# Queries of three rounds before the first weights, value tiles in their used rows, and half a mask in a scheduled place: one change to the start of a three-layer kernel

## The chip, the cores and the metric

The kernel runs on one core of a Trainium2 chip. Its five engines (TensorE, called PE in the profile; VectorE, DVE; ScalarE, ACT; GpSimd, POOL; SyncE, SP) each take their own list of instructions in order and wait for each other with semaphores. All loads and stores of the stretch looked at here are issued by SP on one DMA queue that feeds 16 DMA engines. The metric is the time of one execution in microseconds of the device; lower is better.

## What is computed

```python
scores = scale * np.matmul(q, k.transpose(0, 1, 3, 2))          # batch 4, 8 heads, 576 tokens, head size 64
mask_local = (rel >= 0) & (rel < 32)                            # heads 0 to 3
mask_strided = (rel >= 0) & (pos[None, :] % 32 == pos[:, None] % 32)   # heads 4 to 7
...
x = softmax(where(mask, scores, -1e9)) @ v                      # 2304 tokens x 512
h = x @ w_in; r = np.maximum(h, 0.0)                            # 512 x 2048
x = (s * (r * r) + b) @ w_out                                   # 2048 x 512
logits = x @ w_gate; e_idx = np.argmax(logits, axis=1)          # one of 8 experts for each token
out[mask] = gate_w * eom * (np.maximum(x[mask] @ w1[e], 0.0) @ w2[e])
```

## The kernel before

**Units and rounds.** The 2304 tokens are cut into five units: unit 0 has 256 tokens, units 1 to 4 have 512. Attention comes in 30 rounds (`GROUPS`). A round of kind L holds blocks of 64 local queries with 96 keys each; kinds P and T hold the strided heads (P the first residue rows of a batch, T the rest). A round is: scores on PE into a pair of PSUM banks (line 574 puts the mask there as a product with the identity, line 579 adds query times key), the maximum on DVE (line 605), for the first nine rounds one exponential for each block on ACT (line 613), the sum's reciprocal and the division on DVE (lines 627 to 630), transposes on PE (line 648), a copy on ACT (line 654), the product with the values on PE (lines 685 and 687), and two halves of the result, high on ACT (line 714) and low on DVE (line 731), in the tile `xsl`, which is the x of the next layer. Unit 0 needs rounds 0 (L), 1 (L) and 2 (P). Unit 1 needs rounds 3 (L), 4 (L), 5 (T), 6 (T), 7 (L) and 8 (P).

**The dense layers.** A step of unit u and slice fc is 12 products of the first layer into `h` (line 855) and, one step later, 12 products of the second layer into four accumulators (line 885). Between them a chain squares the rectified `h` on ACT (lines 819, 824, 832) and leaves a low half to DVE (line 834). The first steps are: five of unit 0, whose second-layer products come after all five; then ten of unit 1; then the rest of unit 0. So unit 1's first five steps use the ten weight tiles that unit 0's five have used already.

**Weights.** A weight tile arrives as 64-bit numbers (`raw`, 512 KB, line 753). DVE puts together a 32-bit number in three steps (lines 791, 794, 797), the high half is copied by ACT (line 765) or DVE (line 767), and DVE makes the low half (line 778). The order is `WSEQ`: five tiles of the first layer, five of the second, then the rest.

**What sets the order.** A planner (`Order`) runs while the program is built: it keeps a clock for each engine, takes the piece of work that could start first by its own cost figures (with small bonuses), and so writes one list for each engine. The chip only follows these lists. A spawned piece with `after=True` may not be planned before the spawning piece has finished on the planner's clock. SP's list too comes from it: `load_qkv` issues `LOADS` one after the other (k = 0 is queries with keys, k = 1 values), `load_w64` the weights, and `FIRST_LOADS` weaves the first of both by small delays (q a query tile, v a value tile, w a weight). Loads share a pool of 32 slots (`t_w`); in the list a load also waits for the one eight places before it. Where the planner expects PE to be idle it puts in products on a tile of zeros (`warm`, line 1571, and `filler`, line 1582); they read and write nothing that counts.

**The start.** `prep` makes the identity, the local mask and, in a loop over two parts, the two strided masks of batch 0 (part 0 for kind P, part 1 for kind T) on POOL, each followed by a copy on ACT (line 461).

Of the kernel before, what the change touches and what calls it, by code (L numbers as in the profile page):

```python
# [10 lines left out]
AF = mybir.ActivationFunctionType  # L11
# [8 lines left out]
NT, DM, DFF, E, DFE = B * S, H * D, 2048, 8, 1024  # L20
# [14 lines left out]
P = 128  # L35
# [3 lines left out]
LK = QB + STRIDE  # L39
# [51 lines left out]
def steps():  # L91
# [6 lines left out]
GROUPS = [("L", 0, 0, 2), ("L", 0, 2, 2), ("P", 0, 0, 4),  # L98
# [4 lines left out]


def part_of(g):

    kind, b = GROUPS[g][0:2]
    late = kind == "T"
    return FIRST[b] * late, CLS if late else FIRST[b], RES[b][late]


def dims(g):

    if GROUPS[g][0] == "L":
        return QB, LK
    j0, j1, r = part_of(g)
    return r * (j1 - j0), QB if GROUPS[g][0] == "P" else r * j1
# [22 lines left out]
MB = [(QB if b < 3 else RES[b][0] * FIRST[b], RES[b][1] * CLS) for b in range(B)]  # L140
# [23 lines left out]


WQ, WV = 1024, 768
LOADS = [(0, 0), (1, 0), (0, 1), (2, 0), (1, 1), (3, 0), (2, 1), (3, 1)] + [(g, k) for g in range(4, len(GROUPS)) for k in range(2)]
FIRST_LOADS = "qwqvwqvwqvwvw"
LATE_Q = [k / 1000 for k, x in enumerate(FIRST_LOADS) if x in "qv"]
LATE_W = [k / 1000 for k, x in enumerate(FIRST_LOADS) if x == "w"]  # L170


def widths(g):
    kind, b, i0, n = GROUPS[g]
    qw, w = dims(g)
    if kind == "L":
        return 2 * (n * QB + n * QB + STRIDE), n * 2 * P
    if kind == "P":
        return 2 * 2 * n * QB, n * P
    return 2 * (n * qw + QB - qw + n * w), n * 2 * P  # L180
# [118 lines left out]
def op(*engs, waits=(), dep=True, on=(), late=0.0):  # L299
    return engs, waits, dep, on, late  # L300
# [6 lines left out]
def body(ctx, tc, qkv, w12, moe_s, moe_b, wg, e12, out):  # L307
    nc = tc.nc
# [10 lines left out]
    at = at_ctx.enter_context(tc.tile_pool(name="at", bufs=2))  # L319
# [15 lines left out]
    mh = wp.tile([P, sum(MB[0])], F32R, name="mh", tag="w")  # L335
# [14 lines left out]
    wgt = const.tile([P, KD, 4 * E], F32, name="wgt")  # L350
# [3 lines left out]
    wt = const.tile([P, E], F32, name="wt")  # L354
# [11 lines left out]
    o = Order()  # L366
# [71 lines left out]
    def prep():  # L438
        nc.vector.memset(ones, 1.0)
        nc.vector.memset(zero.bitcast(F32), 0.0)  # L440
        one = mx.tile([P, P], F32, name="one", tag="r", bufs=NR)
        nc.gpsimd.memset(one, 0.0)
        nc.gpsimd.affine_select(out=one, in_=one, pattern=[[-1, P]], compare_op=ALU.not_equal,
                                fill=1.0, base=0, channel_multiplier=1)
        nc.scalar.activation(out=ident_r, in_=one, func=AF.Copy)
        nc.scalar.activation(out=minus_r, in_=one, func=AF.Copy, scale=-1.0)
        nc.vector.tensor_reduce(out=pick, in_=one.rearrange("p (k e) -> p e k", e=4 * E), axis=AX.X, op=ALU.add)
        mf = mx.tile([P, 2 * LK + sum(MB[0])], F32, name="mf", tag="r", bufs=NR)
        loc = mf[:, 0:2 * LK].rearrange("p (i k) -> p i k", i=2)
        nc.gpsimd.memset(loc, 0.0)  # L450
        for a in range(0, P, QB):
            nc.gpsimd.affine_select(out=loc[a:a + QB], in_=loc[a:a + QB], pattern=[[0, 2], [-1, LK]], compare_op=ALU.is_ge,
                                    fill=NEG, base=STRIDE, channel_multiplier=1)
            nc.gpsimd.affine_select(out=loc[a:a + QB], in_=loc[a:a + QB], pattern=[[0, 2], [1, LK]], compare_op=ALU.is_gt,
                                    fill=NEG, base=0, channel_multiplier=-1)
        nc.gpsimd.memset(loc[:, 0, 0:STRIDE], NEG)
        nc.scalar.activation(out=mk[:, 0:2 * LK], in_=mf[:, 0:2 * LK], func=AF.Copy)
        for k in range(2):
            make_masks(0, (k,), mf[:, 2 * LK:])
            a, b = k * MB[0][0], MB[0][0] + k * MB[0][1]  # L460
            nc.scalar.activation(out=mh[:, a:b], in_=mf[:, 2 * LK + a:2 * LK + b], func=AF.Copy)
        nc.gpsimd.memset(wgt, 0.0)
        nc.gpsimd.iota(wt, pattern=[[-1, E]], base=E, channel_multiplier=0, allow_small_or_imprecise_dtypes=True)
        o.clock["DVE"] = 1.7
        o.clock["DMA"] = 1.4
        o.clock["POOL"] = 5.5
        o.clock["ACT"] = 5.5
        o.clock["PE"] = 1.7
        ev_mk.t = 4.2
        ev_mp.t = 5.8  # L470
        ev_mb[0].t = 8.5


    def make_masks(b, parts, m):

        for k in parts:
            j0, j1, r, w = ((0, FIRST[b], RES[b][0], MB[b][0]), (FIRST[b], CLS, RES[b][1], MB[b][1]))[k]
            c = k * MB[b][0]
            v, nj = m[:, c:c + w], j1 - j0
            used = r * j1  # L480
            nc.gpsimd.memset(v[:, 0:used], 0.0)
            if used < w:
                nc.gpsimd.memset(v[:, used:], NEG)
            for a in range(0, P, QB):
                x = v[a:a + QB, 0:used].rearrange("p (r j) -> p r j", j=j1)
                for pattern, base, sign in (([[-nj, r], [-1, j1]], j0, 1), ([[nj, r], [0, j1]], nj - 1, -1)) + ((([[-nj, r], [0, j1]], 0, 1),) if j0 else ()):
                    nc.gpsimd.affine_select(out=x, in_=x, pattern=pattern, compare_op=ALU.is_ge, fill=NEG, base=base, channel_multiplier=sign)

    ev_mb = [Ev() for _ in range(B)]
    ev_mp = Ev()  # L490
    ev_md = [Ev() for _ in range(B)]

    def masks(b):
        yield op(("POOL", 8.0), waits=[ev_k[0]] if b == 1 else [ev_md[b - 1]])
        t = at_pool.tile([P, sum(MB[1])], F32, name="xt", tag="xt", bufs=1)
        make_masks(b, (0, 1), t)
        yield op(("ACT", 0.35))
        nc.scalar.activation(out=xm[:, 0:sum(MB[b])], in_=t[:, 0:sum(MB[b])], func=AF.Copy)
        o.set(ev_mb[b])
        if b + 1 < B:  # L500
            o.spawn(masks(b + 1))

    ev_k = [Ev() for _ in range(NU * NF)]
    ev_qkv = {x: Ev() for x in LOADS}
    at_pool = at
# [16 lines left out]
    def load_qkv(at):  # L522
        g, k = LOADS[at]
        w = widths(g)[k]
        yield op(("DMA", 0.0014 * w), waits=([t_qe if g < NEARLY else t_qv] if k == 0 else []) + ([t_w] if g < NEARLY else []),
                 late=LATE_Q[at] if at < len(LATE_Q) else P_QKL)
        if g < NEARLY:
            t = wp.tile([P, w], F32, name="qkv", tag="w")
        else:
            t = at_pool.tile([P, (WQ, WV)[k]], F32, name="qkv", tag=("qk", "vv")[k], bufs=NQV)[:, 0:w]  # L530
        wq, wv = widths(g)
        nc.sync.dma_start(out=t, in_=qkv[g, k * P * wq:P * (wq + k * wv)].rearrange("(p n) -> p n", n=w))
        qkvs[g, k] = t
        o.set(ev_qkv[g, k], o.fin + DMA_LAT)
        if at + 1 < len(LOADS):
            o.spawn(load_qkv(at + 1))

    def attn(g):
        kind, b, i0, n = GROUPS[g]
# [208 lines left out]
    def load_w64(at):  # L748
        j = WSEQ[at]
        yield op(("DMA", 1.46), waits=[t_rw, t_w], late=LATE_W[at] if at < len(LATE_W) else 0.0)  # L750
        t = wp.tile([P, 512, 2], I32, name="raw64", tag="w")
        fc, n = divmod(j, 2)
        nc.sync.dma_start(out=t, in_=w12[fc].bitcast(I32)[:, n * 1024:(n + 1) * 1024].rearrange("p (f t) -> p f t", t=2))
        raw64[j] = t
        o.set(ev_r[j], o.fin + DMA_LAT)
        if at == 12:
            o.spawn(consts())
        if at + 1 < 2 * NF:
            o.spawn(load_w64(at + 1))

    def split(raw, n, ev, hi_tok, by_pe=None):
        yield op(("ACT", 0.63), ("DVE", 0.42, P_DVE if n not in DVE_FIRST else P_DVE1), waits=[t_w])
# [794 lines left out]
    def consts():  # L1557
        yield op(("DMA", 1.0))
        nc.sync.dma_start(out=s_sb, in_=moe_s.partition_broadcast(P))
        nc.sync.dma_start(out=b_sb, in_=moe_b.partition_broadcast(P))  # L1560
        with nc.allow_non_contiguous_dma(reason="half of every group of columns"):
            nc.sync.dma_start(out=wgt[:, :, 0:2 * E], in_=wg)
        o.set(ev_g, o.fin + 6.0)
# [36 lines left out]
    n = nc.values_load(ex["li"][0:1, 2:3], min_val=0, max_val=SLOT, skip_runtime_bounds_check_because=why)  # L1600
# [70 lines left out]
```

## Time and profile before

| | |
|---|---|
| median of 3 runs | 713.98 us (713.75 to 714.26) |
| the profiled execution | 713.82 us, its span 712.0 us, 0.16 us under the median |
| TensorE | 700.6 us busy, 98% of the span |
| VectorE, ScalarE | 316.8 us (44%), 274.6 us (39%) |
| DMA in the first three of 40 slices (17.8 us each) | 8, 9 and 5 tenths busy, 324, 402 and 222 GB/s |
| mean granted TensorE clock | 0.999 |

The trace is that of one execution. Its times count from the start of the span; 1.8 us of the execution lie around the span. "Busy" for PE is no proof of useful work, since the zero products count as busy too.

### The profile page before, as it was taken

How to read it: one execution, taken by the hardware profiler on the slowest of the kernel's cores; microseconds unless marked ns; L12 is line 12 of the kernel's file. 1: busy time of each engine (PE TensorE's matmuls, PEld its weight loads, DVE VectorE, ACT ScalarE, POOL GpSimd, SP SyncE). 2: the span in 40 equal slices, each digit the busy share in tenths (PEclk: the TensorE clock that was granted, in tenths of full speed). 3: DMA queues.
4: the chain of work that ended last, by engine and by line, in shares of the span. 5: the costliest groups of instructions: out<-in, count | busy, mean ns of one | idle time of the engine just before them, and what ended most of it. 6: DMA issues, size and time to landing. Idle time of an engine off the chain costs nothing.

```text
span 712.0 us, 11678 instructions
## 1 busy us (share of the span) xinstructions
PE 700.6 (98%) x4616; PEld 593.2 (83%) x4616; DVE 316.8 (44%) x725; ACT 274.6 (39%) x582; POOL 26.2 (4%) x111
## 2 busy tenths in 40 slices
PE   9999999999999999999999999999999999999996
PEld 8887888997877777877778878888899999899995
DVE  6998887753244352254341144312475326221220
ACT  5875546554344343354333554333221212121110
POOL 5000000220000000000000000000000000000000
PEclk9999999999999999999999999999999999999999
DMA  8957313314031112025200142101413971001001
GB/s 324 402 222 270 144 57 144 109 63 142 1 113 46 53 42 83 1 92 74 79 1 1 59 163 91 44 1 57 31 17 98 329 284 68 16 16 44 32 15 48
DMA packets 36076, 68.99 MB, mean 97 GB/s; under 512 B 8877, under 2 KB 16558, under 8 KB 35250
## 3 DMA queue, kind: packets, MB, share of 16 engines
q1 hardware_dynamic: 35890, 68.20, 29.3%
q8 instruction: 37, 0.61, 0.4%
q14 instruction: 21, 0.17, 0.1%
q0 software_dynamic: 128, 0.02, 0.0%
HBM read 56.75 MB, written 11.70 MB: 96 GB/s over the span
## 4 chain that ended last, share of the span: by engine, by line
PE 92%; DMA 4%; DVE 3%; SPq 0%; issue 0%; ACT 0%
PE h L855 27%; PE bk L885 27%; PE h L1217 14%; PE bk L1242 12%; DMA raw<-w 2%; PE bk L687 2%; PE bk L1261 2%; PE bk L579 2%; PE bk L648 2%; DMA qkv<-qkv 1%; PE bk L990 1%; DVE w L794 1%; DVE w L797 1%; PE bk L1532 1%; PE bk L1509 1%; PE bk L1010 0%
## 5 line engine op out<-in xcount | busy, mean ns | idle before, releaser
L855 PE MATMUL h<-xsl,w 128*128 128x512 f32 (+1 forms) x960 | 219.4, 373 | 0.8 <-DVE xsl L731 0.5
L885 PE MATMUL bk<-g,w 128*128 128x512 f32 (+1 forms) x888 | 206.3, 378 | 0.2 <-DVE g L834 0.2
L855 PEld LDWEIGHTS h<-xsl,w 128*128 128x128 f32 x960 | 166.1, 188 | 33.3 <-DVE xsl L731 0.8
L885 PEld LDWEIGHTS bk<-g,w 128*128 128x128 f32 x888 | 156.5, 188 | 31.6 <-issue 2.1
L819 ACT ACTIVATE r<-h 128x512 f32<-128x512 f32 (+1 forms) x80 | 44.5, 556 | 183.8 <-PE h L855 171.8
L834 DVE TENSOR_TENSOR g<-r,g 128x512 fp32r<-128x512 f32 (+1 forms) x75 | 48.9, 653 | 143.7 <-ACT g L832 143.3
L1217 PE MATMUL h<-x,w 128*128 128x384 f32 x576 | 108.9, 338 | 0.0
L1217 PEld LDWEIGHTS h<-x,w 128*128 128x128 f32 x576 | 102.0, 188 | 4.2 <-issue 1.0
L1242 PE MATMUL bk<-w,ht 128*128 128x512 f32 x360 | 89.6, 393 | 0.0
L1170 ACT ACTIVATE ht<-h 128x384 fp32r<-128x384 f32 x48 | 23.6, 491 | 149.0 <-PE h L1217 149.0
L1242 PEld LDWEIGHTS bk<-w,ht 128*128 128x128 f32 x360 | 66.6, 188 | 12.1 <-issue 0.4
L1172 DVE SCALAR_TENSOR_TENSOR ht<-h,ht 128x384 fp32r<-128x384 f32 x48 | 26.8, 558 | 109.4 <-ACT ht L1170 109.3
L824 ACT ACTIVATE r<-r 128x512 f32<-128x512 f32 (+1 forms) x80 | 47.1, 589 | 2.3
L832 ACT ACTIVATE g<-r 128x512 fp32r<-128x512 f32 (+1 forms) x75 | 45.0, 600 | 2.9
L687 PEld LDWEIGHTS bk<-ph,qkv 96*64 96x64 f32 (+4 forms) x576 | 18.5, 137 | 8.9 <-issue 5.3
L687 PE MATMUL bk<-ph,qkv 96*64 96x64 f32 (+7 forms) x576 | 22.2, 226 | 1.3 <-ACT ph L654 1.3
L731 DVE TENSOR_TENSOR xsl<-bk,xsl 128x384 fp32r<-128x384 f32 (+9 forms) x31 | 13.8, 447 | 19.0 <-ACT xsl L714 18.9
L794 DVE SCALAR_TENSOR_TENSOR w<-raw,w 128x512 int32<-128x512 int32 x32 | 22.0, 688 | 0.3
L797 DVE SCALAR_TENSOR_TENSOR w<-raw,w 128x512 int32<-128x512 int32 x32 | 21.9, 685 | 0.2
L778 DVE TENSOR_TENSOR w<-w,w 128x512 fp32r<-128x512 f32 x32 | 21.6, 682 | 0.4 <-ACT w L765 0.2
L654 ACT ACTIVATE ph<-bk 96x768 f32<-96x768 f32 (+10 forms) x27 | 18.3, 677 | 8.3 <-PE bk L648 7.7
L648 PE MATMUL bk<-mk,pr 128*96 128x128 f32 (+5 forms) x142 | 20.6, 273 | 0.7 <-DVE pr L630 0.7
(189 smaller groups left out, 511.7 us busy)
## 6 DMA issues: line engine op xcount, KB each, us to landing
raw<-w SPq DMA_DIRECT2D x32, 512.0 KB, 8.0
qkv<-qkv SPq DMA_DIRECT2D x14, 384.0 KB, 8.5
out<-ob SPq DMA_DIRECT2D x17, 256.0 KB, 2.3
xd<-x SPq DMA_DIRECT2D x4, 1024.0 KB, 4.5
wraw<-e SPq DMA_DIRECT2D x16, 256.0 KB, 2.6
X<-xd SPq DMA_DIRECT2D x4, 1024.0 KB, 8.2
we<-e SPq DMA_DIRECT2D x8, 512.0 KB, 7.4
qkv<-qkv SPq DMA_DIRECT2D x14, 256.0 KB, 4.8
```

The source lines that it names most:

```text
L648: nc.tensor.transpose(out=pt[0:nk, h - hs[0], j, :], in_=src, identity=ident)
L687: nc.tensor.matmul(out=dst, lhsT=lhs, rhs=rhs)
L794: nc.vector.scalar_tensor_tensor(out=a, in0=hi, scalar=-(1 << 30), in1=a, op0=ALU.bitwise_and, op1=ALU.bitwise_or)
L797: nc.vector.scalar_tensor_tensor(out=a, in0=lo, scalar=29, in1=a, op0=ALU.logical_shift_right, op1=ALU.bitwise_or)
L819: nc.scalar.activation(out=r, in_=h, func=AF.Relu)
L824: nc.scalar.activation(out=r, in_=r, func=AF.Square)
L832: nc.scalar.activation(out=gt[:, 0, 0:U], in_=r, func=AF.Copy)
L834: nc.vector.tensor_sub(out=gt[:, 1, 0:U], in0=r, in1=gt[:, 0, 0:U].bitcast(F32))
L855: nc.tensor.matmul(out=h, lhsT=w_t[2 * fc][:, a, c * P:(c + 1) * P], rhs=xt(u, c, x), start=(c == 0 and n == 0), stop=(c == KD - 1 and n = ...
L885: nc.tensor.matmul(out=acc[pu][c], lhsT=w_t[2 * pf + 1][:, a, c * P:(c + 1) * P], rhs=gt[:, x, 0:cols(pu)], start=(first and n == 0), stop ...
L1217: nc.tensor.matmul(out=h, lhsT=w_t["p", 2 * fc][:, a, c * P:(c + 1) * P], rhs=x2[s][:, x, c, :], start=(c == 0 and n == 0), stop=(c == KD ...
L1242: nc.tensor.matmul(out=acc2[q][t][0], lhsT=pbox[0][:, x, t * P:(t + 1) * P], rhs=w_t["p", 2 * pf + 1][:, a, :], start=(pf == 0 and n == 0) ...
```

## The change

Four edits. `LOADS` and `FIRST_LOADS` put the queries of rounds 0, 1 and 2 ahead of everything, then values and weights by turns. The spawns of the next load and of the next weight get `after=False`. A value tile is loaded in the rows that the value product reads: 96 of 128 for kind L, the keys of a residue group (108, 90, 72 or 54) for kind T and its last small round, 128 for kind P. And part 1 of batch 0's strided mask, with two small POOL instructions, moves from `prep` to a piece that the planner places.

```diff
 WQ, WV = 1024, 768
-LOADS = [(0, 0), (1, 0), (0, 1), (2, 0), (1, 1), (3, 0), (2, 1), (3, 1)] + [(g, k) for g in range(4, len(GROUPS)) for k in range(2)]
-FIRST_LOADS = "qwqvwqvwqvwvw"
+LOADS = [(g, k) for k in range(2) for g in range(3)] + [(g, k) for g in range(3, len(GROUPS)) for k in range(2)]
+FIRST_LOADS = "qqqvwvwvwqvwqvwqvwqvwqvwqvw"
...
-        for k in range(2):
-            make_masks(0, (k,), mf[:, 2 * LK:])
-            a, b = k * MB[0][0], MB[0][0] + k * MB[0][1]
-            nc.scalar.activation(out=mh[:, a:b], in_=mf[:, 2 * LK + a:2 * LK + b], func=AF.Copy)
-        nc.gpsimd.memset(wgt, 0.0)
-        nc.gpsimd.iota(wt, pattern=[[-1, E]], base=E, channel_multiplier=0, allow_small_or_imprecise_dtypes=True)
+        make_masks(0, (0,), mf[:, 2 * LK:])
+        nc.scalar.activation(out=mh[:, 0:MB[0][0]], in_=mf[:, 2 * LK:2 * LK + MB[0][0]], func=AF.Copy)
+        o.spawn(masks(0, mf), after=False)
...
-        ev_mb[0].t = 8.5
...
-    def masks(b):
+    def masks(b, mf=None):
+        if b == 0:
+            yield op(("POOL", 3.0))
+            make_masks(0, (1,), mf[:, 2 * LK:])
+            nc.gpsimd.memset(wgt, 0.0)
+            nc.gpsimd.iota(wt, pattern=[[-1, E]], base=E, channel_multiplier=0, allow_small_or_imprecise_dtypes=True)
+            yield op(("ACT", 0.3))
+            nc.scalar.activation(out=mh[:, MB[0][0]:], in_=mf[:, 2 * LK + MB[0][0]:], func=AF.Copy)
+            o.set(ev_mb[0])
+            return
...
-        wq, wv = widths(g)
-        nc.sync.dma_start(out=t, in_=qkv[g, k * P * wq:P * (wq + k * wv)].rearrange("(p n) -> p n", n=w))
+        wq = widths(g)[0]
+        rows = P if k == 0 or GROUPS[g][0] == "P" else dims(g)[1]
+        nc.sync.dma_start(out=t[0:rows], in_=qkv[g, k * P * wq:k * P * wq + rows * w].rearrange("(p n) -> p n", n=w))
...
-            o.spawn(load_qkv(at + 1))
+            o.spawn(load_qkv(at + 1), after=False)
...
-            o.spawn(load_w64(at + 1))
+            o.spawn(load_w64(at + 1), after=False)
```

How this moves instructions shows in the lists of the engines. In the change the lines stand six further down (574 is 580, 753 is 759, 885 is 891, and so on). First SP, from its first load on; `raw` is a weight tile, `qkv` a tile of queries with keys or of values, with rows and columns behind it. Before:

```order
L532 DMA qkv<-qkv 128x576
L753 DMA raw_188<-w 128x1024
L532 DMA qkv<-qkv 128x576
L753 DMA raw_217<-w 128x1024
L532 DMA qkv<-qkv 128x512
L753 DMA raw_245<-w 128x1024
L532 DMA qkv<-qkv 128x1024
L753 DMA raw_285<-w 128x1024
```

And in the change:

```order
L538 DMA qkv<-qkv 128x576 x2
L538 DMA qkv<-qkv 128x1024
L538 DMA qkv<-qkv 96x512
L759 DMA raw_210<-w 128x1024
L538 DMA qkv<-qkv 96x512
L759 DMA raw_261<-w 128x1024
L538 DMA qkv<-qkv 128x512
L759 DMA raw_286<-w 128x1024
```

Round 2's queries (the tile of 1024 columns) were the seventh load and are the third; the first weight was the second load and is the fifth.

The second place is PE from round 0's scores on. `bk` is a PSUM bank pair or bank, `mk` and `mh` hold masks, `pr` probabilities, `ph` their transposes. Before:

```order
L579 MATMUL bk_106<-qkv 64x96 x8
L1571 MATMUL warm<-xsl 128x256 x5
L574 MATMUL bk_110<-mk 128x192 x2
L579 MATMUL bk_110<-qkv 64x96 x8
L1571 MATMUL warm<-xsl 128x256 x13
L648 MATMUL bk_277<-mk,pr 96x128 x4
L1571 MATMUL warm<-xsl 128x256 x5
L685 MATMUL bk_278<-ph,qkv 64x64 x8
L648 MATMUL bk_315<-mk,pr 96x128 x4
L574 MATMUL bk_110<-mh,mk 128x256 x2
L579 MATMUL bk_110<-qkv 64x64 x16
```

And in the change:

```order
L585 MATMUL bk_106<-qkv 64x96 x8
L580 MATMUL bk_110<-mk 128x192 x2
L585 MATMUL bk_110<-qkv 64x96 x8
L580 MATMUL bk_114<-mh,mk 128x256 x2
L585 MATMUL bk_114<-qkv 64x64 x16
L1577 MATMUL warm<-xsl 128x256 x13
L654 MATMUL bk_297<-mk,pr 96x128 x4
```

The scores of rounds 0, 1 and 2 now stand one behind the other; before, round 2's (the 16 products of 64 columns) came after round 0's value product.

The third place is PE around the end of unit 0's first layer, where the second layer begins (`gw` is its input). Before:

```order
L855 MATMUL h<-xsl,w 128x256 x12
L1582 MATMUL bk_789<-xsl 128x256 x4
L648 MATMUL bk_110<-mk,pr 108x128 x6
L687 MATMUL bk_789<-ph,qkv 64x60 x8
L687 MATMUL bk_789<-ph,qkv 64x20 x4
L1582 MATMUL bk_788<-xsl 128x256 x4
L885 MATMUL bk_903<-gw,w 128x258 x3
L885 MATMUL bk_904<-gw,w 128x258 x3
L885 MATMUL bk_905<-gw,w 128x258 x3
L574 MATMUL bk_925<-xm,mk 128x256 x2
L579 MATMUL bk_925<-qkv 64x64 x16
```

And in the change:

```order
L1588 MATMUL bk_761<-xsl 128x256 x9
L654 MATMUL bk_110<-mk,pr 108x128 x6
L1588 MATMUL bk_760<-xsl 128x256 x7
L693 MATMUL bk_761<-ph,qkv 64x60 x8
L693 MATMUL bk_761<-ph,qkv 64x20 x4
L580 MATMUL bk_110<-xm,mk 128x256 x2
L585 MATMUL bk_110<-qkv 64x64 x16
L654 MATMUL bk_365<-mk,pr 96x128 x6
L1588 MATMUL bk_761<-xsl 128x256 x7
L693 MATMUL bk_760<-ph,qkv 64x64 x12
L861 MATMUL h<-xsl,w 128x256 x12
L1588 MATMUL bk_365<-xsl 128x256 x11
```

Behind the last row stand the second layer's products, as before. The scores of round 8 (the 16 products), round 7's transposes and value product, and the last 12 products of unit 0's first layer now come ahead of the second layer, with 34 zero products of line 1588 among them (9, 7, 7 and 11) where there were 8. Round 8's scores lie in `bk_110`, whose bank the second layer takes over; before they lay in a bank that it does not take.

## Rows read from the trace of the kernel before

**Rows 1.** The page: busy time of TensorE, and ACT's group of line 654.

```profile
PE 700.6 (98%) x4616; PEld 593.2 (83%) x4616; DVE 316.8 (44%) x725; ACT 274.6 (39%) x582; POOL 26.2 (4%) x111
...
L654 ACT ACTIVATE ph<-bk 96x768 f32<-96x768 f32 (+10 forms) x27 | 18.3, 677 | 8.3 <-PE bk L648 7.7
```

**Rows 2.** Waits of PE from 62 to 712 us: total, times, longest.

```profile
PE bk L885 <- DVE g L834: 0.2, 1, 0.2
```

**Rows 3.** Timeline of PE, 54.6 to 64.5 us: start, duration; idle before in brackets.

```profile
55.50 1.66 PE L855 MATMUL h<-xsl,w 128*128 128x512 f32 x6
57.40 0.50 PE L855 MATMUL h<-xsl,w 128*128 128x512 f32 x1 [0.24 <-ACT xsl L714]
58.43 4.15 PE L855 MATMUL h<-xsl,w 128*128 128x512 f32 x17 [0.54 <-DVE xsl L731]
62.42 0.76 PE L1582 MATMUL bk<-xsl 128*128 128x256 f32 x5
63.02 0.39 PE L885 MATMUL bk<-g,w 128*128 128x512 f32 x1
63.57 1.19 PE L885 MATMUL bk<-g,w 128*128 128x512 f32 x4 [0.16 <-DVE g L834]
```

**Rows 4.** Two stretches: PE, PEld, DVE, ACT, POOL busy; granted clock, DMA share, GB/s.

```profile
24.00:42.00 18.00, 16.99 (x233) 15.25 (x232) 16.61 (x38) 15.12 (x61) 0.38 (x6) 1.00 1.04 398
42.00:60.00 18.00, 16.89 (x202) 14.80 (x203) 17.45 (x41) 11.70 (x45) 0.00 (x0) 1.00 0.36 116
```

**Rows 5.** Timeline of DVE, 56.5 to 64 us.

```profile
58.08 0.30 DVE L731 TENSOR_TENSOR xsl<-bk,xsl 128x144 fp32r<-128x144 f32 x1
...
60.56 0.42 DVE L791 TENSOR_SCALAR w<-raw 128x512 int32<-128x512 int32 x1
60.90 0.69 DVE L797 SCALAR_TENSOR_TENSOR w<-raw,w 128x512 int32<-128x512 int32 x1
61.50 0.68 DVE L794 SCALAR_TENSOR_TENSOR w<-raw,w 128x512 int32<-128x512 int32 x1
```

**Rows 6.** Timeline of SP, from 0 us: issue of the first weight.

```profile
1.26 0.42 SPq L753 DMA_DIRECT2D raw<-w  x1
```

**Rows 7.** DMA issues from 0 to 2 us: count, KB each, us from issue to landing.

```profile
qkv<-qkv SPq DMA_DIRECT2D x2, 288.0 KB, 2.8
raw<-w SPq DMA_DIRECT2D x1, 512.0 KB, 5.3
```

**Rows 8.** Timeline of PE, 0 to 60 us.

```profile
5.41 0.92 PE L579 MATMUL bk<-qkv 64*64 64x96 f32 x16
...
7.49 0.57 PE L574 MATMUL bk<-mk 128*128 128x192 f32 x2
7.99 0.92 PE L579 MATMUL bk<-qkv 64*64 64x96 f32 x16
...
13.77 0.69 PE L579 MATMUL bk<-qkv 64*64 64x64 f32 x32
...
26.14 1.59 PE L855 MATMUL h<-xsl,w 128*128 128x256 f32 x12
...
42.12 0.88 PE L687 MATMUL bk<-ph,qkv 108*64 108x60 f32 x24 [1.12 <-ACT ph L654]
...
43.50 1.26 PE L885 MATMUL bk<-gw,w 128*128 128x258 f32 x9
```

**Rows 9.** Timeline of DVE, 0 to 60 us.

```profile
9.46 0.16 DVE L627 TENSOR_SCALAR sm<-sm 128x4 f32<-128x4 f32 x1
...
9.86 0.65 DVE L630 TENSOR_TENSOR pr<-pr,sm 128x384 f32<-128x384 f32 x1
...
26.06 0.41 DVE L731 TENSOR_TENSOR xsl<-bk,xsl 128x256 fp32r<-128x256 f32 x1
```

**Rows 10.** Timeline of ACT, 7.4 to 9.5 us.

```profile
7.91 0.34 ACT L613 ACTIVATE pr<-bk,sm 128x96 f32<-128x96 f32 x1
...
8.24 0.33 ACT L613 ACTIVATE pr<-bk,sm 128x96 f32<-128x96 f32 x1
```

## The prediction

> **What bounds the kernel now.** The page comes first: PE is busy for 98% of the span [rows 1], so the time falls only where PE does something useless or waits. The list of PE's waits says where that is: from 62 us to the end it waits 0.2 us in all [rows 2]. So the start alone counts. PE's timeline gives the place at which the start ends: the second product of unit 1's first second-layer step, at 63.57 us [rows 3]. I call it the mark. In both kernels the same useful work stands ahead of it (rounds 0 to 8, five steps of unit 0, two first-layer blocks of unit 1), and the order behind it stays nearly the same, so the kernel gains what the mark gains. The profiled execution (713.82 us) is 0.16 us under the median of 713.98 us; differences are taken over to the median unchanged.
>
> What holds the mark? The windows: from 24 to 60 us DVE is busy 16.61 and 17.45 of 18 us, ACT 15.12 and 11.70 [rows 4]. DMA is full until 42 us (398 GB/s, share 1.04) but not after (116 GB/s). In the last stretch PE waits for the x of unit 1: round 8's result comes out of DVE at 58.08 + 0.30 = 58.38 us [rows 5], and PE's eighth product goes on at 58.43 us [rows 3].
>
> **The change, part by part.**
>
> *Queries first.* Rounds 0, 1 and 2 need 288 + 288 + 512 = 1,088 KB. In the kernel before, the first 800 KB (round 0's queries and the first weight) had landed at 1.26 + 5.3 = 6.55 us [rows 6, 7]. At 398 GB/s the next 288 KB take 0.74 us, so round 2's queries are there at 7.3 us. Round 0's scores end at 5.41 + 0.92 = 6.33 us as before [rows 8]. Round 1 (masks 0.5 us from start to start, scores 0.92) ends at about 7.7. Round 2: two mask products 256 wide instead of 192, 0.67; then 16 score products, 0.69 us at 13.77 in the trace, but twice eight took 0.92 each early on; I take 1.1 (bounds 0.69 and 1.84). So they end at 9.4 us, where they ended at 13.77 + 0.69 = 14.46. From there to unit 0's x the trace has 26.06 + 0.41 - 14.46 = 12.0 us [rows 8, 9]. The same chain gives x at 21.4 us, 5.1 us earlier (bounds 20.6 and 22.2 by the 16 products; the later weights leave DVE less to do in between, round 1's softmax stands closer ahead). Round 5's queries, whose scores now stand ahead of unit 0's first product, end at 5,980 KB: 6.55 + 5,180 x 1.024 / 398 = 19.9 us, in time.
>
> *Weights later.* The first weight ends at 1,792 KB, 9.1 us instead of 6.55. The order of DVE puts its first step behind round 1's softmax, so nothing waits. The ninth ends at 12,064 KB, 35.5 us, long before DVE takes it. What this costs is DVE work that is left for later.
>
> *DVE from 21.4 us on.* Its order in the change, from unit 0's last x half to the low half of the ninth weight (the fourth of the second layer): 21 full steps of weights (lines 800, 803, 784), 0.60 us each by 60.90 to 61.50, 12.6 us; ten short ones (797, 773), 0.34 each by 60.56 to 60.90, 3.4 us [rows 5]; ten softmax steps of six rounds, 5,728 columns, by the same 0.60 for 512, 6.7 us; six sum pairs, 9.46 to 9.86, 0.40 each, 2.4 us [rows 9]; x halves, 1,904 columns, 2.2 us; five g halves of 256, 1.5 us. Sum 28.8 us. DVE idles 1.39 of 18 us (7.7%) in 24 to 42 and 0.55 (3.1%) in 42 to 60 [rows 4]; weighted by the time spent in each, 6.2%: 30.7 us. So the ninth weight is whole at 52.2 us. Two of the five second-layer steps then remain, 24 products at 1.26 / 9 = 0.14, 3.4 us [rows 8]. Unit 1 begins at 55.6 us; before it began at 55.50 [rows 3]. The 5.1 us are spent: the change does rounds 7 and 8 and the weights' backlog inside them.
>
> *Unit 1's waits go.* Round 8's last x half stands only two DVE steps behind that ninth weight, at about 53.3 us, and so ahead of unit 1's first product, where it was 2.9 us behind it (58.38 against 55.50). Before, 17 products took 62.42 - 58.43 = 3.99 us, 0.235 each, so 24 should have ended at 55.50 + 5.63 = 61.13; they ended at 62.42: 1.29 us lost. And 63.02 to 63.57 between two products instead of 0.235: another 0.32 us for g's low half [rows 3]. In the change g's low half comes with slack: two blocks of PE hide that chain everywhere behind 62 us [rows 2]. The five zero products stay (0.60 us).
>
> *Sum.* Mark in the change: 55.6 + 5.63 + 0.60 + 0.24 = 62.1 us, against 63.57: 1.5 us less.
>
> *Fewer value rows.* The first nine rounds load 504 KB less, 1.3 us at 398 GB/s. Hidden: nothing waits for a load after 21 us, and after 42 us DMA is two thirds idle [rows 4]. If DMA were to gate, it would be a gain of at most 1.3 us. *Mask.* The POOL work moves by some microseconds and is needed at 21 us; the ACT copy now stands behind round 2's exponentials. Nothing, as long as POOL has it done then. *The loops' `after=False`* only acts through these orders.
>
> *Zero products.* 34 instead of 8 stand ahead of the second layer, five in 0.60 us [rows 3], so 4.1 us that PE spends whether it waits there or not. This is the price that the bound below contains.
>
> [...]
>
> **The rivals.**
>
> *PE alone decides (more gain).* From 26.14 to 55.50 us PE had 29.4 us, less the wait of 1.12 and eight zero products (0.96): 27.3 useful. In the change the corresponding first product stands behind round 5's scores, at about 23.0 us (x at 21.4, three zero products, about 1.2 us of scores); round 3's transposes come on top, 0.6, and the zero products, 4.1: 55.0 us at the earliest, mark 61.5, 2.1 us less, 711.9. For it: 5.1 us of lead. Against: it allows no wait at all where there were 1.12 us. If waits and zero products overlapped more kindly and x came at 20.6, 711.1.
>
> *No change.* If DVE idles twice as much as its share says (3.8 us), unit 1 begins at 57.4, mark 63.9: 714.3, within the bound. For it: the order mixes its chains more tightly, a round's division waits for ACT's last exponential.
>
> *The second layer opens late (slower).* It takes over the bank of round 8's scores and so waits for that round's eight exponentials on ACT. Compared with the list ahead of 43.50, where the second layer began [rows 8], ACT has eight exponentials more at 0.33 [rows 10], one copy of 0.68 [rows 1] and five smaller pieces, taken at 0.45 between these two: 5.6 us, and at ACT's share of 15.12 in 18 us [rows 4] 6.6 us. If the earlier x doesn't let ACT start its part earlier, the layer opens at 50.1 instead of the 46 or so that the sum leaves room for; 60 products and round 8's transposes and value product, 8.4 + 1.3, and the mark is 59.8 + 6.5 = 66.3: 716.7. It decides from an opening at 48.8 on. Against: x leads by 5.1 us, and ACT idled 2.9 us in 24 to 42.
>
> [...]
>
> **How the numbers follow.** 0.2% is 1.43 us, about what a measurement of this kernel can tell from no change. Forecast (1 to 2 us less) 0.45, about two thirds of it beyond the bound; PE alone 0.16; no change 0.24; late opening 0.12; clock 0.03. So faster 0.46, same 0.39, slower 0.15. Predicted 713.98 - 1.5 = 712.5 us. The range goes from 710.9 (PE alone with the early x) to 715.4 (half of the late opening's price); the forecast's own is 711.9 to 713.2.
>
> **What would show it.** Right: round 2's scores ending near 9.4, unit 0's x near 21.4, its first product near 23, the second layer opening near 46, unit 1 beginning near 55.6 with no wait for `xsl`, and no wait of PE behind 62 us. Wrong: x later than 23; DVE idle above 3.5 us between 21 and 52; the opening ending on an ACT exponential at 49 or later; a granted clock under 1.00; or a PE wait after the mark because two weights fewer are ready there.

## The result and the profile after

The change takes 719.51 us (median of 6 runs, 717.75 to 720.85) against 713.87 us (6 runs) before: a ratio of 1.0072, 95% interval 1.0049 to 1.0095. It is slower by about 5.6 us, where 1.5 us less was forecast, and outside the stated range of 710.9 to 715.4 us. The profiled execution is the slowest of the six (720.85 us, span 719.1); its last DVE instruction starts at 712.83 us instead of 705.47, 7.4 us later.

The two windows that answer to [rows 4], and two slices of the first (columns as there):

```profile
24.00:42.00 18.00, 13.50 (x168) 12.21 (x169) 9.48 (x20) 9.02 (x41) 0.26 (x4) 0.81 1.03 279
42.00:60.00 18.00, 17.28 (x216) 15.92 (x214) 17.11 (x38) 13.40 (x53) 0.00 (x0) 1.00 0.67 218
30.00:36.00 6.00, 4.86 (x58) 4.45 (x59) 2.66 (x5) 1.08 (x2) 0.00 (x0) 0.54 1.03 277
36.00:42.00 6.00, 6.00 (x74) 5.53 (x73) 3.69 (x8) 4.49 (x21) 0.13 (x2) 0.89 1.03 281
```

Look at the last two columns first. The DMA engines are as busy as before (share 1.03), but they move 279 GB/s where they moved 398. DVE, the engine on which the forecast was built, is busy for 9.48 of 18 us instead of 16.61: it starves. The granted clock, 1.00 in both rows of [rows 4], is 0.54 from 30 to 36 us (0.50 for most of it).

The list of PE's waits, 0 to 62 us, says whom PE waits for:

```profile
PE bk L585 <- DMA qkv<-qkv: 5.0, 2, 3.6
PE warm L1577 <- DVE xsl L440: 1.4, 1, 1.4
```

From 62 us on the list is empty, as forecast. PE's timeline, to be held against [rows 3, 8]:

```profile
8.50 1.13 PE L585 MATMUL bk<-qkv 64*64 64x64 f32 x32
9.56 3.14 PE L1577 MATMUL warm<-xsl 128*128 128x256 f32 x13
...
22.60 0.52 PE L1588 MATMUL bk<-xsl 128*128 128x256 f32 x3
22.95 0.55 PE L580 MATMUL bk<-mh,mk 128*128 128x324 f32 x2
24.92 0.79 PE L585 MATMUL bk<-qkv 64*64 64x108 f32 x24 [1.42 <-DMA qkv<-qkv]
25.64 0.98 PE L861 MATMUL h<-xsl,w 128*128 128x256 f32 x6
...
31.14 1.36 PE L585 MATMUL bk<-qkv 64*64 64x108 f32 x24 [3.57 <-DMA qkv<-qkv]
...
55.73 2.40 PE L891 MATMUL bk<-gw,w 128*128 128x258 f32 x18
...
64.91 5.66 PE L861 MATMUL h<-xsl,w 128*128 128x512 f32 x24
70.41 0.76 PE L1588 MATMUL bk<-xsl 128*128 128x256 f32 x5
71.00 2.91 PE L891 MATMUL bk<-g,w 128*128 128x512 f32 x12
```

And of DVE, the last half of unit 0's x:

```profile
22.71 0.42 DVE L737 TENSOR_TENSOR xsl<-bk,xsl 128x256 fp32r<-128x256 f32 x1
```

Read it downward. Round 2's scores end at 9.6 us, as forecast (9.4). Unit 0's x is whole at 22.71 + 0.42 = 23.13 us, 1.7 us later than forecast and past the "later than 23" that was to show the forecast wrong. This delay comes ahead of the first wait for a load. The value tiles don't make it: e5 below has it too. The 13 zero products behind round 2's scores take 0.21 us each, as the first ones of the execution do, where later ones take 0.12, and round 0's transposes stand behind them. Then PE stands 1.42 us for the queries of round 5 and 3.57 us for those of round 6. From there everything is late: second layer at 55.73, unit 1 at 64.91, the mark (the second product of the step, at 71.00 + 0.24) at 71.24 against 63.57. Unit 1's 24 products do run without a wait, in 5.66 us (5.63 was forecast), so the wait that the change was to remove is gone. It was worth little beside what came.

Why are the queries late? The rows on DMA for 24 to 30 us, of the kernel before and then of the change:

```profile
DMA packets 741, 2.42 MB, mean 404 GB/s; under 512 B 82, under 2 KB 82, under 8 KB 740
```

```profile
DMA packets 501, 1.68 MB, mean 280 GB/s; under 512 B 55, under 2 KB 55, under 8 KB 500
...
qkv<-qkv SPq DMA_DIRECT2D x1, 512.0 KB, 13.8
```

The engines never pause; they finish 501 packets in the time of 741. The packets themselves became slower, those of full tiles too: in these 6 us the packets of 4,096 bytes, which at that time only full tiles have, took 242 ns on average instead of 162. A tile of 512 KB lands 13.8 us after its issue, its time in the queue included.

### The profile page after: what moved, and what is told of

It reads as the page before. It is cut to its first block, busy times and chain, and to the rows that moved or that the text cites. A ratio compares the mean times of both kernels' runs of the same rounds, so it can differ in the third digit from the quotient of the medians.

```text
span 719.1 us, 11692 instructions
## 1 busy us (share of the span) xinstructions
PE 705.1 (98%) x4625; PEld 598.3 (83%) x4625; DVE 317.4 (44%) x725; ACT 274.9 (38%) x582; POOL 26.5 (4%) x111
## 4 chain that ended last, share of the span: by engine, by line
PE 94%; DMA 4%; ACT 1%; DVE 0%; issue 0%; SPq 0%
PE h L861 28%; PE bk L891 28%; PE h L1223 14%; PE bk L1248 12%; DMA qkv<-qkv 4%; PE bk L693 3%; PE bk L1267 2%; PE bk L654 2%; PE bk L585 2%; PE bk L996 1%; PE bk L1538 1%; PE bk L1515 1%; PE bk L1016 0%; PE bk L1235 0%; PE bk L1410 0%; ACT pr L619 0%
## 5 line engine op out<-in xcount | busy, mean ns | idle before, releaser
L585 PEld LDWEIGHTS bk<-qkv 64*64 64x64 f32 x608 | 14.5, 145 | 12.9 <-DMA qkv<-qkv 5.7
L585 PE MATMUL bk<-qkv 64*64 64x96 f32 (+4 forms) x608 | 20.1, 262 | 5.0 <-DMA qkv<-qkv 5.0
L660 ACT ACTIVATE ph<-bk 96x768 f32<-96x768 f32 (+9 forms) x26 | 18.0, 691 | 15.6 <-PE bk L654 15.1
```

Of the source, the lines that this page charges most:

```text
L585: nc.tensor.matmul(out=sc[p * QB:(p + 1) * QB, h, at_i, :], lhsT=q[h * D:(h + 1) * D, p, i * qs:i * qs + QB], rhs=k[h * D:(h + 1) * D, p, ...
```

## The experiments

**Theory R**: loads of fewer than 128 rows slow every transfer that is in flight with them. **Rival O**: the new order of the loads brings queries and weights late. Four kernels, the edit of each against the change or the kernel before:

```
e1  the change:  rows = P                                     # all value tiles whole again
e2  before:      + rows = P if k == 0 or GROUPS[g][0] == "P" else dims(g)[1]
e3  the change:  rows = dims(g)[1] if k == 1 and GROUPS[g][0] == "L" else P
e4  loads alone: 10 phases of 16 loads of 1024 columns into 16 buffers, from partition 0
    rows (first, second load, ...): 128,128  96,96  128,96  108,108  128,108  128,112  128,64  128,72  128,90  128,128
```

> The change with its value tiles loaded in all 128 rows again; everything else, and every instruction list, as in the change. Theory R (tiles of fewer than 128 rows slow every transfer that is in flight with them): DMA back near 400 GB/s from 6 to 36 us, round 6's scores wait under 0.5 us, granted clock 1.00 from 30 to 36, time 711 to 714, as the sum of the prediction had it. Theory O (the new order of the loads is what costs): DMA stays near 300 GB/s and the time at 717 to 721.

Measured: 712.95 us against 713.86, ratio 0.999 (0.998 to 1.0). The 5.6 us are gone, and the DMA rate and the clock of the first window are back:

```profile
24.00:42.00 18.00, 15.96 (x240) 14.42 (x242) 14.70 (x34) 15.13 (x61) 0.13 (x2) 1.00 1.03 406
42.00:60.00 18.00, 17.68 (x196) 16.23 (x189) 17.65 (x40) 9.73 (x34) 0.00 (x0) 1.00 0.19 63
```

Two parts of the expectation were missed. From 6 to 12 us the rate is 314 GB/s (309 in the change), so what is slow there isn't the value tiles. And round 6's scores still wait 1.55 us, where under 0.5 was expected. PE's timeline has this wait, and the 13 zero products that took 3.14 us in the change:

```profile
9.55 2.27 PE L1577 MATMUL warm<-xsl 128*128 128x256 f32 x13
...
26.34 0.79 PE L585 MATMUL bk<-qkv 64*64 64x108 f32 x24 [1.55 <-DMA qkv<-qkv]
```

> The kernel before with the used rows alone, order of loads and mask as before. Theory R: DMA falls to about 300 GB/s from 9 us on, PE waits for queries appear between 20 and 35 us, time 717 to 722. Theory O: DMA stays near 400 GB/s, time 713 to 714.5.

Measured: 718.29 us, ratio 1.007 (1.0052 to 1.0089). The used rows alone, on the old order, cost 4.4 us; the rate in 18 to 36 us is 290 to 304 GB/s, PE waits 2.6 us for round 4's queries, and the granted clock falls after it:

```profile
18.00:24.00 6.00, 2.98 (x25) 2.64 (x23) 4.48 (x12) 4.13 (x21) 0.00 (x0) 0.97 1.05 290
24.00:30.00 6.00, 5.83 (x81) 5.11 (x82) 3.71 (x7) 2.23 (x12) 0.26 (x4) 0.50 1.04 297
```

O falls: the old order suffers alike, the new one with whole tiles doesn't.

> The change with used rows for the local rounds alone (96 of 128), kinds T in 128 rows. Within theory R: if 96 rows are what slows the transfers, about as slow as the change, 717 to 721; if only row counts that 16 does not divide (108, 90, 72) do, 711 to 714. Theory O: 717 to 721.

Measured: 715.17 us, ratio 1.0016 (1.0005 to 1.0028), 2.2 us above e1 and between the two ranges expected. The 96 rows of the L rounds are a third of the cost.

> Loads alone: ten groups of 16 loads of 1024 columns, every second one with fewer rows (all 128; all 96; then 128 with 96; all 108; then 128 with 108, 112, 64, 72, 90; all 128), nothing else computed. Theory R: the groups with 128 rows alone run at 390 to 410 GB/s, the ones with 96 or 108 at 270 to 330 GB/s, and the 128-row loads between them are slow too. Theory O: every group runs at 380 GB/s or more, up to the bytes that a smaller tile leaves out.

Measured: from the first to the last of 16 landings (15 gaps), per tile: 128 rows 1.28 us, 96 rows 1.53 us, 108 rows 1.43 us; in turn with whole tiles, 96: 1.46, 108: 2.04, 112: 1.53, 64: 1.56, 72: 1.39, 90: 1.44. Every mixture is slower than whole tiles alone although it moves less; the pair 128 and 108, which is what rounds 5 and 6 have beside the weights, is the worst. A tile of 96 rows alone takes longer than a whole one. R holds without a kernel around it.

Next, where the partial tiles cost, and how. Edits against the change, e8 again loads alone:

```
e5  rows = P if k == 0 or GROUPS[g][0] == "P" or g < NEARLY else dims(g)[1]   # used rows from round 9 on
e6  for _ in range({5: 10, 6: 27}.get(g, 0)):                                 # ahead of the score products
        nc.tensor.matmul(out=two_banks(toks)[:, 0, 0:2 * P], lhsT=zero[:, 0:P], rhs=zero, start=False, stop=False)
e7  rows = dims(g)[1] if k == 1 and GROUPS[g][0] == "T" else P
e8  phases of 16: [0:128] of 1024 columns, [0:128] of 768, [0:96], [32:128], [0:64], [0:32] + [64:96], [0:64] + [64:96], ...
```

> The change, but the value tiles of rounds 0 to 8 are loaded in all 128 rows and only those of rounds 9 to 29 in their used rows; nothing is left out. Theory R (loads of fewer than 128 rows slow every transfer that is in flight with them, which costs time only where PE waits for transfers, in the first 54 us): as e1, 712.9 us, 712.3 to 713.8, no wait for queries over 2 us. If partial loads cost where they stand, whatever surrounds them: 21 of the 30 rounds still have them, so more than half of the 6.6 us is left, 716 to 718 us.

Measured: 712.82 us, ratio 0.998 (0.9969 to 0.9991), no wait for queries. As R has it: 21 rounds with partial tiles cost nothing once PE no longer waits for transfers. This version is measurably faster than the kernel before, by 1.1 us; of the others only e10 below is.

> The change, with 10 zero products put ahead of round 5's score products and 27 ahead of round 6's, each added into the bank that the scores go to, so that PE works while it waits for queries; nothing is left out. The queries still come late: the first h product stays at 25 to 26 us and the DMA's throughput at 280 GB/s. Theory C (the half clock after the wait is part of the cost): the granted clock stays at 1.00 in 24 to 42 us, where the change lost 6 x 0.46 + 6 x 0.11 = 3.4 us of PE time, and the time falls to about 716.1 us. Theory W (late transfers alone set the second layer, the clock only fills time in which PE would wait anyway): the clock stays up too, but the second layer still opens near 55.7 and the time stays at 718 to 720.5 us.

Measured: 720.01 us, ratio 1.0071 (1.0044 to 1.0098). The time is the one that W named, but the run isn't the test that it was meant to be. In its profile the clock falls earlier, behind a wait of 2.3 us for round 3's queries, and is 0.50 from 15.89 to 26.13 us; the first h product comes at 28.34 us (25 to 26 was expected). And the 27 zero products hold up the scores that they stand ahead of: round 6's start at 33.42 us, right behind them and without a wait for queries, where the change has them at 31.14:

```profile
24.00:42.00 18.00, 18.00 (x222) 16.97 (x221) 11.00 (x27) 10.50 (x44) 0.26 (x4) 0.94 1.04 298
...
30.11 3.38 PE L582 MATMUL bk<-xsl 128*128 128x256 f32 x27
33.42 0.79 PE L587 MATMUL bk<-qkv 64*64 64x108 f32 x24
```

What tells Theory C from Theory W is the stretch from the start of round 6's scores to the mark, in which PE does the same work (435 products) in all these kernels with the new order. Its row in e1, e3, e6, the change and e7, then the part of the change's with a low clock, then the same stretch of the old order, before and in e2:

```profile
26.34:63.70 37.36, 36.54 (x435) 33.28 (x436) 33.20 (x73) 25.43 (x91) 0.13 (x2) 1.00 0.60 222
28.84:66.17 37.33, 36.51 (x435) 33.27 (x435) 34.20 (x75) 26.67 (x97) 0.13 (x2) 1.00 0.68 206
33.42:70.72 37.30, 36.49 (x435) 33.27 (x435) 33.19 (x73) 24.73 (x86) 0.13 (x2) 1.00 0.61 190
31.14:71.24 40.10, 39.27 (x435) 35.75 (x436) 33.39 (x73) 24.89 (x86) 0.13 (x2) 0.92 0.65 193
27.63:66.48 38.85, 38.02 (x435) 34.70 (x435) 33.29 (x73) 24.77 (x86) 0.13 (x2) 0.96 0.61 218
...
31.14:37.36 6.22, 6.21 (x64) 5.71 (x64) 2.92 (x7) 2.12 (x7) 0.00 (x0) 0.50 1.03 277
...
29.38:63.57 34.19, 31.93 (x376) 28.09 (x375) 32.32 (x73) 25.06 (x89) 0.00 (x0) 1.00 0.67 239
34.11:68.29 34.18, 31.91 (x376) 28.08 (x375) 32.09 (x72) 25.06 (x89) 0.00 (x0) 1.00 0.76 229
```

At full clock the stretch takes 37.3 us with whole tiles and with partial ones (e5 and e10 have 37.3 too), and 34.2 in the old order, with either. So behind round 6's scores the slow transfers cost nothing. The half clock does: 2.7 us in the change, 1.5 in e7, where it lasts shorter. W falls for this stretch, and C is right: the half clock is part of the cost. These are single executions; how much the clock costs in the median isn't shown.

> The change, with used rows for the T rounds' value tiles alone (108, 90 and 72 rows) and all 128 rows for the L rounds'; nothing is left out. If the two kinds simply add, e3 (L alone: 715.2, 2.2 us above e1) leaves 4.3 us of the 6.6 us: 717.3 us. If only the number of partial tiles in the first 54 us counts: T has two of the seven (rounds 5 and 6), so about 714.8 us. In either case a wait of PE for round 6's queries of over 2 us is expected, as round 5's tile of 108 rows lands just ahead of them.

Measured: 716.20 us, ratio 1.0022 (1.0002 to 1.0042), 3.3 us above e1, between the two numbers expected; PE waits 5.0 us for queries, three times. L and T alone give 2.2 + 3.3 = 5.5 of the 6.6 us that the two together cost.

> Loads alone; the whole computation is left out and the output is zeros. Eleven phases of 16 loads each: 128 rows of 1024 columns; 128 rows of 768; rows 0 to 95; rows 32 to 127; rows 0 to 63; two loads of 32 rows (0 to 31 and 64 to 95) per tile; two loads of 64 and 32 rows (0 to 63, 64 to 95) per tile; whole tiles in turn with those; 112 rows; whole tiles in turn with tiles of twice 32 rows; 128 rows again. [...] Theory K (only the split of the rows over engines counts): 64 rows and 32 + 32 rows take the same time.

Measured per tile, in the steady part of a phase: 128 rows 1.28 us; 128 rows of 768 columns 0.96; rows 0 to 95 1.48; rows 32 to 127 1.37; rows 0 to 63 1.28; twice 32 rows 1.03 (0.51 a load); 64 + 32 rows 1.62; 112 rows 1.72; whole tiles in turn with the halved ones 1.75 (64 + 32 rows) and 1.42 (twice 32), slower than whole tiles alone in both cases. Three stretches of DVE's timeline, where one instruction follows each landing (128x768; rows 0 to 63; the two loads of 32 rows):

```profile
32.26 0.14 DVE L328 COPY z<-ld 32x1 f32<-32x1 f32 x1 [0.82 <-DMA ld<-e]
33.22 0.14 DVE L328 COPY z<-ld 32x1 f32<-32x1 f32 x1 [0.82 <-DMA ld<-e]
...
108.22 0.14 DVE L328 COPY z<-ld 32x1 f32<-32x1 f32 x1 [1.14 <-DMA ld<-e]
109.50 0.14 DVE L328 COPY z<-ld 32x1 f32<-32x1 f32 x1 [1.14 <-DMA ld<-e]
...
124.72 0.14 DVE L328 COPY z<-ld 32x1 f32<-32x1 f32 x1 [0.35 <-DMA ld<-e]
125.23 0.14 DVE L328 COPY z<-ld 32x1 f32<-32x1 f32 x1 [0.37 <-DMA ld<-e]
```

Fewer columns shorten a load in proportion here (0.96 against 1.28 us for three quarters of them); fewer rows don't. Rows 0 to 63 take the 1.28 us of a whole tile for half its bytes, and the same count of rows, placed half below and half above 64, takes 1.03 us. So which partitions are written counts here, and the equal times that Theory K has for the two aren't what was measured. Whether the 1.03 us are the price of two issues isn't shown; one issue took SP 0.42 us in the kernel before [rows 6]. Loads of 96 and 112 rows from partition 0 take 1.48 and 1.72 us, longer than the 1.28 of the 64 rows that they contain; no run shows why. (e11 below, in phases that overlap, has 1.02 for 64 rows.)

The last three, on the order's own gain and on the row counts:

```
e9  e5, in filler():  if ev_x[0].t is not None and ev_k[8].t is None: return   # no L1588
e10 e5, with make_masks(0, (k,), ...) for both k in prep(), as in the kernel before
e11 loads alone: 13 phases of 8 loads from partition 0: 128 127 126 125 124 120 112 104 96 80 64 32 128 rows
```

> e5 (the change, with the value tiles of rounds 0 to 8 in all rows) without the 29 zero products that stand between unit 0's x and the end of the second layer's unit 0; nothing is left out. Rival Z (in e5 the zero products hold PE up; the second layer opens at 47.8 only because 11 of them, 1.48 us, stand directly ahead of it): it opens at 46 us or earlier, the first layer of unit 1 begins near 55, the mark comes 1.5 to 2 us earlier and the time falls to about 711.2 us. Theory D (DVE and ACT set the opening; the zero products fill waits): the waits of PE show up in the same places, the opening stays within 0.5 us of 47.8, and the time stays at 712.0 to 713.6, or goes up if the granted clock falls in those waits.

Measured: 716.16 us, ratio 1.0024 (1.0011 to 1.0037). Z falls. The edit took out 42 zero products (the expectation's 29 was a miscount: 37 stand ahead of the end of unit 0, 5 behind it). PE waits 3.0 us between 37 and 46 us where the zero products stood, and then:

```profile
36.00:42.00 6.00, 3.91 (x62) 3.31 (x60) 5.25 (x15) 5.58 (x25) 0.00 (x0) 0.92 1.02 343
42.00:48.00 6.00, 5.10 (x67) 4.16 (x67) 4.59 (x10) 2.90 (x12) 0.00 (x0) 0.50 0.81 290
48.00:54.00 6.00, 4.58 (x22) 4.32 (x21) 4.38 (x11) 2.87 (x14) 0.00 (x0) 0.50 0.01 5
```

The granted clock is 0.50 through the opening of the second layer, which comes at 51.61 us. Zero products in PE's waits are worth 3.3 us here. The loss goes with the clock: the one execution of e9 with a mean granted clock of 0.996 took 713.18 us, the seven at 0.986 to 0.991 took 715.08 to 717.07.

> e5 with the whole mask of batch 0 made ahead of the schedule, as in the kernel before; nothing is left out. The prediction put this edit at nothing. If so: 712.8 us, within 0.1% of e5. If the mask's place matters (its ACT copy ahead of round 0's exponentials, its POOL work ahead of x): the first h product comes more than 0.5 us later than e5's 24.1 and the time rises above 713.6 us.

Measured: 712.91 us, ratio 0.9985 (0.9976 to 0.9994): as e5, and the first h product isn't later (22.70 us against 24.12). The mask's place is worth nothing that can be measured, as predicted.

> Loads alone; the whole computation is left out and the output is zeros. Thirteen phases of 8 loads of 1024 columns each, from partition 0: 128, 127, 126, 125, 124, 120, 112, 104, 96, 80, 64, 32 and 128 rows. [...] Theory B (bytes): times in proportion to the rows. From e4 and e8, 96 rows take 1.5 us, 112 rows 1.7 us and 64 rows 1.28 us.

Measured between landings: 127 rows 19.8 us, 126 rows 1.44, 125 rows 3.90, 124 rows 4.83 (later up to 9), 120 rows 1.94, 112 rows 1.66, 104 rows 2.20, 96 rows 1.59, 80 rows 1.39, 64 rows 1.02, 32 rows 0.35, 128 rows 1.28. From 126 on neighbouring phases overlap, so for 112, 96 and 64 rows the figures of e4 and e8 are the cleaner ones. Two gaps of 127 rows and two of 125 in DVE's timeline:

```profile
33.24 0.14 DVE L325 COPY z<-ld 32x1 f32<-32x1 f32 x1 [19.10 <-DMA ld<-e]
53.04 0.14 DVE L325 COPY z<-ld 32x1 f32<-32x1 f32 x1 [19.66 <-DMA ld<-e]
72.84 0.14 DVE L325 COPY z<-ld 32x1 f32<-32x1 f32 x1 [19.66 <-DMA ld<-e]
...
195.42 0.14 DVE L325 COPY z<-ld 32x1 f32<-32x1 f32 x1 [3.76 <-DMA ld<-e]
199.32 0.14 DVE L325 COPY z<-ld 32x1 f32<-32x1 f32 x1 [3.76 <-DMA ld<-e]
```

127 x 4,096 B in 19.8 us are 26 GB/s, 125 rows make 131, five times that, and 124 rows 105, four times. The busy share of the 16 DMA engines, which the page gives in tenths, follows: 0 in the slices of 26 and 27 GB/s, 3 in those of 126 to 131, 2 in those of 105; whole tiles have 1.03 at 413 (e8). A sixteenth of 413 is 26 GB/s, so 127, 125 and 124 rows keep about one, five and four of the engines at work (an estimate from these rates). How many of them a load of another row count uses isn't shown.

## Why the prediction was wrong

*The step that failed* is the one on the value rows: "The first nine rounds load 504 KB less, 1.3 us at 398 GB/s. Hidden: nothing waits for a load after 21 us". It took the DMA rate of the kernel before as a constant and let only the bytes change; the same 398 GB/s dates "Round 5's queries ... 19.9 us, in time". With partial tiles in flight the rate is 277 to 331 GB/s in each 6 us from 12 to 42 us (399 to 411 in e1), and round 5's queries are there at 24.9 us, round 6's at 31.1. No rival had it either: "no change" and "late opening" priced DVE and ACT, and the DMA was named only as something that might give a gain. The edit's cost is e1 against the change, 6.6 us, and 4.4 us on the old order.

*Where the time goes from there.* The two profiles put the mark at 71.24 and 63.70 us, 7.5 apart. Round 6's scores start when their queries are there, 4.8 us later (31.14 against 26.34); the other 2.7 us lie in the stretch behind them, where the granted clock is 0.50 until 37.36. That DVE starves is a consequence: from 22 to 42 us it waits 5.4 us for scores of PE. The chance of 0.03 that the forecast gives to the clock had no run behind it: the kernel before shows 1.00 from 24 to 60 us [rows 4]. What the runs showed in its place is the half clock of the change, behind waits for loads at 23 to 31 us. Between 37 and 46 us, where PE waits 3.0 us in e9, zero products keep it at 1.00 in e5; without them it is 0.50 from 42 to 54 us.

*What held.* Round 2's scores at 9.6 us (9.4), in e1 unit 0's x at 21.8 (21.4) and its first product at 22.86 (23.0), no xsl wait in unit 1, no PE wait behind the mark, nothing for the mask (e10).

*The order's own gain* was over-sized. With whole tiles the second layer opens at 48.19 us in e1 (forecast 46), unit 1 begins at 57.36 (55.6), and the mark's second product starts at 63.70, 0.1 us later than before. The forecast had 28.8 us of DVE work and 1.9 of idle time from x to the ninth weight. In e1 and in e5 this stretch is:

```profile
21.84:54.54 32.70, 30.39 (x422) 27.56 (x421) 29.05 (x65) 24.54 (x98) 0.26 (x4) 1.00 0.74 284
23.11:54.18 31.07, 30.30 (x422) 27.54 (x421) 29.00 (x65) 24.19 (x98) 0.26 (x4) 1.00 0.79 268
```

The work is right, to 0.3 us. In e1 the failed term is the idle time, 3.65 us, of which 1.4 wait for round 6's scores: their queries come late with whole tiles too, so "nothing waits for a load after 21 us" fails here as well. In e5 they are in time and DVE idles 2.07 us, but x, the start of the sum, is 1.7 us late. The forecast took x's chain from the old order, where products of 256 columns took 0.12 us; in the change they took 0.21 until past 12 us, and e5 runs alike there (71 products from 6 to 12 us, 72 in the change). If round 6's queries had been in time in e1, the mark would be at 62.1 us, as forecast (an estimate: 1.55 us less, the 37.4 us behind kept). The rival "no change" has e1's numbers (3.8 us of idle, unit 1 at 57.4) partly by luck: it gave mixed chains and waits for ACT as the reason, and 1.4 us are a wait for a load. In the profiles of e1, e5 and e10 the last DVE instruction starts 0.2, 0.6 and 0.5 us earlier than 705.47; the medians say 0.9 to 1.1 us less, of which only e5 and e10 exclude no change. The end of the span lies 4.8 to 6.1 us behind that instruction from one profile to the next, whatever the kernel, so single spans can't settle the rest.

*Left open:* why 112 rows take longer than 108 and 96 longer than 64; how the number of rows and their place among the partitions make a load slow, and its neighbours with it; and why TensorE's early pace has ended by 5.3 us in e3's profile (16 score products in 0.56 us) and lasts past 12 us in the change's (0.92 at 5.41 and 6.93). That e1 waited for round 6's queries and e5 didn't has two parts: e5's PE came to them 1.2 us later, by that pace, and the queries were there earlier: round 6's scores start at 25.99 us without a wait, at 26.34 behind one in e1.

## What to carry to other kernels

Bytes saved by dropping partitions from a load were not time saved here: alone, every tile of 80 to 127 rows that was measured took longer than one of 128 (1.37 us and more against 1.28). Load whole 128-row tiles, padding included, and save columns instead (0.96 against 1.53 us for the same 384 KB); 127 rows cost fifteen times as much as 128 (19.8 against 1.28 us). When an edit touches the shape of a transfer, the rate of everything in flight with it is a term of the sum (242 ns a packet of a full tile instead of 162), and the stage with a DMA share of 1.03 had no cover for it: PE waited 5.0 us for queries. Check what fills an engine's planned waits before taking it out: the zero products looked like 4 us of waste and were worth 3.3 us. And to split a delay between two causes, compare executions from the first instruction behind the last late load: here that stretch had one length in five of them, and what was longer had a low clock.

## What the runs showed of the hardware

A DMA share of 1.03 to 1.04 was read at 280 and at 406 GB/s alike: here busy engines said nothing of their rate. Whole 512 KB tiles land every 1.28 us alone; in turn with tiles of 108 rows a tile lands every 2.04 us on average. One row less than 128 raised a load from 1.28 to 19.8 us. At the start the clock row can't be trusted: in the change it says 1.00 from 6 to 12 us, and there zero products of 256 columns take 0.21 us each, as they do in e3 between 23.3 and 24 us, where the row says 0.50. At the other level they take 0.12 us.
